# Batch 0's attention by halves of the tokens, with its states loaded by GpSimd's queue

## The chip, the cores and the metric

The kernel runs on one core of a Trainium2 chip. Its engines are TensorE (PE; PEld is its weight load), VectorE (DVE), ScalarE (ACT), GpSimd (POOL) and SyncE (SP), and 16 DMA engines serve the queues of SP, ACT and POOL. The metric is the device time of one execution in microseconds (us), median of several runs.

## The reference, cut to what matters

Two stages follow each other. First, for each of 8 batches and 8 heads, 512 tokens `x` and 32 states `state`, both of width 64, attend to each other in both directions. Then the result, 8 x (512 + 32) = 4352 rows of 512, goes through a wide layer with the activation h * erf(softplus(h)).

```python
# x: (8, 8, 512, 64), state: (8, 8, 32, 64); scale = 1/8
scores = scale * x @ state^T            # (B, H, 512, 32)
a = exp(scores - max over the 32); a /= sum + 1e-9
xread = a @ state                       # tokens read the states
scores2 = scale * state @ x^T           # (B, H, 32, 512)
a2 = exp(scores2 - max over the 512); a2 /= sum + 1e-9
sread = a2 @ x                          # states read the tokens
rows = concat(xread, sread)             # -> (4352, 512)
h = rows @ w_in                         # w_in (512, 2048), float64 in memory
g = h * erf(softplus(h))
out = g @ w_out                         # w_out (2048, 512), float64 in memory
```

Two things that the kernel does with this matter here. It never forms `xread`: it multiplies the states by `w_in` first (m = state @ w_in) and then the weights `a` by m. And it turns the float64 weights into float32 itself, on ScalarE and VectorE, piece by piece ("i" a piece of w_in, "o" a piece of w_out).

## The kernel before

Batch 0's tokens come in four chunks of 128, on two queues in turn, and the states follow on SP's queue. Then the first weight pieces are fetched, on SP as well.

```python
for c in range(NC):
    (nc.scalar, nc.sync)[c % 2].dma_start(
        out=x_t[0][:, c], in_=x[0, :, P * c:P * c + P].rearrange("h p d -> p h d"))
for e in range(2):
    nc.sync.dma_start(out=st[:, 0, D * e:D * e + D],
                      in_=state[0].rearrange("(i e) n d -> e i n d", e=2)[e])
```

`attention0` is the attention of batch 0. The tokens are turned on TensorE (so that the width lies on the partitions), copied from PSUM, multiplied by the states, turned back by VectorE, and become weights. `between` holds what is put between the steps.

```python
def attention0(between):
    xt = x_t[0]
    xT = att.tile([P, NI, S], F32, name="xT")
    xp = [ps_o.tile([P, S], F32, name="o%d" % i) for i in range(3)]
    xp.append(ps_h.tile([P, S], F32, name="h"))
    for c in 1, 0, 2, 3:
        if c == 2:
            warm(3)                      # filler products of the identity
        for i in range(NI):              # L304
            nc.tensor.transpose(out=xp[i][:, P * c:P * c + P],
                                in_=xt[:, c, 2 * i:2 * i + 2, :], identity=ident)
    for i in range(NI):                  # L307: 0 and 2 on ScalarE, 1 and 3 on VectorE
        (nc.scalar.copy, nc.vector.tensor_copy)[i % 2](xT[:, i, :], xp[i])
    states(range(1), ps_h, "h")          # turns the states (L182), copies them (L183)
    s2 = scored(0, xT)                   # L197: two PSUM tiles, one for each head of a pair
    between[0]()
    both = att.tile([P, NI, S], F32, name="xT")
    sc = att.tile([P, 2, S], F32, name="sc")
    a = states_weights(0, s2, both)      # L217 turn, L219 maximum, L221 subtract, L222 exp
    for e in range(2):
        nc.scalar.copy(sc[:, e], s2[e])
    between[1]()
    z1 = sums(a)                         # L228
    between[2]()
    normalise(a, z1)                     # L232, L233, L235
    for e in range(2):
        nc.vector.transpose(out=aT[0][:, e], in_=both[:, e])    # L321
    ...
```

A weight piece takes two passes on ScalarE (L144, L146) and three on VectorE (L147 to L149); `on_act` and `on_dve` place them, and the third VectorE pass lets the next piece be fetched. `mixed_part` forms m (L421, copies L423 and L424). `first0` (L714) multiplies m by the turned weights `aT[0]`: TensorE's first product for the wide layer. After it come `soft` (L718), `keep_h` (L721), `erf` (L724), `times` (L727) and the product with w_out (`some0`, L550).

```python
def after_scores():
    warm(32)
    on_act("i", 0)
def before_sums():
    on_act("i", 1)
    on_dve("i", 0, [0, 1])
def amid_sums():
    on_dve("i", 0, [2])
    on_act("o", 0, [0])
    m_t[0, 0] = mix.tile([P, 2, gw], F32, name="m")
    mixed_part(0, 0, 0, 2, nc.scalar.copy, nc.scalar.copy)
    warm(5)
rest = attention0((after_scores, before_sums, amid_sums))
...
first0(0, 0, g0[0])
first0(0, 1, g0[0])
on_dve("i", 1)
soft(0, g0)
...
```

For all of this `in_order` keeps the instructions of TensorE, VectorE, ScalarE and SP in the order of the program. GpSimd is left out of it: in the kernel before, it makes constants and the identity and nothing else.

Of the kernel before, what the change touches and what calls it, by code (L numbers as in the profile page):

```python
# [8 lines left out]
F32 = mybir.dt.float32  # L9
U32 = mybir.dt.uint32  # L10
ALU = mybir.AluOpType
ACTF = mybir.ActivationFunctionType
AX = mybir.AxisListType
# [3 lines left out]
def kernel(  # L17
# [17 lines left out]
    nc = tc.nc  # L35
    B, H, S, D = x.shape
    Ns = state.shape[2]
    d_model, d_ff = moe_w_in.shape
    P = 128
    NI = H // 2  # L40
    NC = S // P
# [5 lines left out]
    scale = 1.0 / (D ** 0.5)  # L47
# [4 lines left out]
    xin = ctx.enter_context(tc.tile_pool(name="xin", bufs=1))  # L52
    att = ctx.enter_context(tc.tile_pool(name="att", bufs=1))
    small = ctx.enter_context(tc.tile_pool(name="small", bufs=2))
    keep = ctx.enter_context(tc.tile_pool(name="keep", bufs=2))
# [3 lines left out]
    ps_at = ctx.enter_context(tc.tile_pool(name="ps_at", bufs=2, space=PSUM))  # L59
    ps_h = ctx.enter_context(tc.tile_pool(name="ps_h", bufs=2, space=PSUM))  # L60
    ps_o = ctx.enter_context(tc.tile_pool(name="ps_o", bufs=1, space=PSUM))

    ident = const.tile([P, P], F32, name="ident")
# [41 lines left out]

    st = const.tile([P, B, P], F32, name="st")
    x_t[0] = xin.tile([P, NC, H, D], F32, name="x")
    for c in range(NC):
        (nc.scalar, nc.sync)[c % 2].dma_start(
            out=x_t[0][:, c], in_=x[0, :, P * c:P * c + P].rearrange("h p d -> p h d"))  # L110
    for e in range(2):
        nc.sync.dma_start(out=st[:, 0, D * e:D * e + D],
                          in_=state[0].rearrange("(i e) n d -> e i n d", e=2)[e])

    def load_st():
        for h in range(H):
# [49 lines left out]
    def warm(n):  # L166

        for _ in range(n):
            last = nc.tensor.matmul(out=spare[:, 0:P], lhsT=ident, rhs=ident, start=True,
                                    stop=True)  # L170
        return last
# [3 lines left out]
    aT = {}  # L175

    def states(bs, pool=ps_at, name="at"):


        ps = pool.tile([P, len(bs), P], F32, name=name)  # L180
        for k, b in enumerate(bs):
            last = nc.tensor.transpose(out=ps[:, k], in_=st[:, b, :], identity=ident)  # L182
        nc.scalar.copy(st[:, bs[0]:bs[-1] + 1, :], ps)  # L183
        return last

    over = lambda t: t.unsqueeze(2).to_broadcast([P, NC * NI, Ns])
# [3 lines left out]
    def scored(b, xT):  # L190


        s2 = [ps_at.tile([P, S], F32, name="at") for _ in range(2)]
        for i in reversed(range(NI)):
            for e in range(2):
                r, q = slice(D * e, D * e + D), slice(Ns * i, Ns * i + Ns)
                on_pe = nc.tensor.matmul(out=s2[e][q, :], lhsT=st[r, b, q], rhs=xT[r, i, :],  # L197
                                         start=True, stop=True)
        marks.append(on_pe)
        return s2  # L200
# [10 lines left out]
    def states_weights(b, sc, both):  # L211

        aT[b] = keep.tile([P, 2, S], F32, name="aT")
        a = both[:, 0:2].rearrange("p e (k n) -> p e k n", n=Ns)
        m1 = small.tile([P, 2, NC * NI], F32, name="m1")
        for e in range(2):
            nc.vector.transpose(out=both[:, e], in_=sc[e])  # L217
        for e in range(2):
            nc.vector.reduce_max(out=m1[:, e], in_=a[:, e], axis=AX.X)  # L219
        for e in range(2):  # L220
            nc.vector.tensor_tensor(a[:, e], a[:, e], over(m1[:, e]), op=ALU.subtract)  # L221
            nc.scalar.activation(out=a[:, e], in_=a[:, e], func=ACTF.Exp, scale=scale)  # L222
        return a

    def sums(a):
        z1 = small.tile([P, 2, NC * NI], F32, name="z1")
        for e in range(2):
            nc.vector.reduce_sum(out=z1[:, e], in_=a[:, e], axis=AX.X)  # L228
        return z1

    def normalise(a, z1):
        nc.vector.tensor_scalar(z1, z1, 1e-9, None, op0=ALU.add)  # L232
        nc.vector.reciprocal(z1, z1)  # L233
        for e in range(2):
            nc.vector.tensor_tensor(a[:, e], a[:, e], over(z1[:, e]), op=ALU.mult)  # L235

    def largest(sc):
        m2 = small.tile([P, 2], F32, name="m2")
        for e in range(2):
            nc.vector.reduce_max(out=m2[:, e:e + 1], in_=sc[:, e], axis=AX.X)  # L240
        nc.vector.tensor_scalar(m2, m2, -scale, None, op0=ALU.mult)
        return m2

    def weigh_tokens(sc, m2, a2):

        z2 = small.tile([P, 2], F32, name="z2")
        for e in range(2):
            nc.scalar.activation(out=a2[:, e], in_=sc[:, e], func=ACTF.Exp, bias=m2[:, e:e + 1],
                                 scale=scale, accum_out=z2[:, e:e + 1])
        return z2  # L250

    def inverse(z):
        nc.vector.tensor_scalar(z, z, 1e-9, None, op0=ALU.add)
        nc.vector.reciprocal(z, z)

    def turn_weights(a2):
        a2T = att.tile([P, 2, NC, P], F32, name="sc")
        for e in range(2):
            ps = ps_at.tile([P, NC, P], F32, name="at")
            for c in range(NC):  # L260
                nc.tensor.transpose(out=ps[:, c, :], in_=a2[:, e, P * c:P * c + P],
                                    identity=ident)
            nc.scalar.copy(a2T[:, e], ps)
        return a2T
# [27 lines left out]
    def attention0(between):  # L292

        xt = x_t[0]
        xT = att.tile([P, NI, S], F32, name="xT")
        xp = [ps_o.tile([P, S], F32, name="o%d" % i) for i in range(3)]
        xp.append(ps_h.tile([P, S], F32, name="h"))
        for c in 1, 0, 2, 3:  # L300
            if c == 2:
                warm(3)
            for i in range(NI):
                nc.tensor.transpose(out=xp[i][:, P * c:P * c + P],  # L304
                                    in_=xt[:, c, 2 * i:2 * i + 2, :], identity=ident)
        for i in range(NI):
            (nc.scalar.copy, nc.vector.tensor_copy)[i % 2](xT[:, i, :], xp[i])  # L307
        states(range(1), ps_h, "h")
        s2 = scored(0, xT)
        between[0]()  # L310
        both = att.tile([P, NI, S], F32, name="xT")
        sc = att.tile([P, 2, S], F32, name="sc")
        a = states_weights(0, s2, both)
        for e in range(2):
            nc.scalar.copy(sc[:, e], s2[e])
        between[1]()
        z1 = sums(a)
        between[2]()
        normalise(a, z1)
        for e in range(2):  # L320
            nc.vector.transpose(out=aT[0][:, e], in_=both[:, e])  # L321

        def rest():
            a2 = both[:, 2:4]
            m2 = largest(sc)
            yield
            z2 = weigh_tokens(sc, m2, a2)
            inverse(z2)
            yield
            a2T = turn_weights(a2)  # L330
            yield
            read_tokens(0, a2T, z2)
            yield

        return rest()
# [304 lines left out]
    def begins(b):  # L640
        return 1 - b % 2
# [48 lines left out]
    def fetch():  # L690
        if len(made) < len(pieces):
            kind, j = w = pieces[len(made)]
            made[w] = (weights_in if kind == "i" else weights_out)(j)

    def on_act(kind, j, ks=range(2)):
        for k in ks:
            made[kind, j][0][k]()

    def on_dve(kind, j, ks=range(3)):
        for k in ks:  # L700
            made[kind, j][1][k]()
            if k == 2:
                fetch()
# [25 lines left out]
    def group():  # L729
        return [act.tile([P, 4, S], F32, name=n) for n in ("s", "hs")]  # L730
# [3 lines left out]
        fetch()  # L734
    warm(8)

    def after_scores():
        warm(32)
        on_act("i", 0)

    def before_sums():
        on_act("i", 1)
        on_dve("i", 0, [0, 1])

    def amid_sums():
        on_dve("i", 0, [2])
        on_act("o", 0, [0])
        m_t[0, 0] = mix.tile([P, 2, gw], F32, name="m")
        mixed_part(0, 0, 0, 2, nc.scalar.copy, nc.scalar.copy)
        warm(5)  # L750

    rest = attention0((after_scores, before_sums, amid_sums))
    g0 = group()

    def some0(g, gT, rs, ts):
# [112 lines left out]
    xT, _ = turn_x(1)  # L868
# [7 lines left out]
    turn = attention(1, xT)  # L876
# [40 lines left out]
    at = [combine_a(1)]  # L917
# [12 lines left out]
    for b in range(1, B + 1):  # L930
# [4 lines left out]
        for g, (first, second) in enumerate(groups):  # L935
# [5 lines left out]
            if b + 1 < B:  # L941

                late = b == 1
                if g == late:
                    side[6 if late else 6] = (lambda: behind(marks, next, turn)) if late else \
                        lambda old=turn: (next(old), behind(marks, next, turn))
                    turn = attention(b + 1)
# [6 lines left out]
                if g > 1:  # L954
                    o = g - 2 ^ begins(b + 1)
# [56 lines left out]
```

## Time and profile before

| | |
|---|---|
| median of 3 runs | 732.24 us (732.22 to 732.41) |
| profiled span | 730.7 us |
| first product of the wide layer (L714) | 22.10 us |
| first product with w_out (L550) | 31.01 us |
| first weight piece in use (ScalarE, L144) | 11.49 us |
| DMA of the first two chunks and states | 256 KB a chunk, 32 KB for each half of the states |

The busy line gives each engine's time, share of the span and instructions; the DMA line gives the busy share of the DMA engines in 40 slices of the span, in tenths. A timeline has one instruction or a merged run of the same kind per line: start, length, engine, source line, operation, tile written from tile read, and in brackets how long the engine had been idle before it and what released it. A float32 product appears as two instructions on TensorE, a transpose as one. Overlapping lengths are usual, since an engine takes up an instruction before the one ahead has ended; the distance between starts is what an instruction costs in a row of them.

### The profile page before, as it was taken

How to read it: one execution, taken by the hardware profiler on the slowest of the kernel's cores; microseconds unless marked ns; L12 is line 12 of the kernel's file. 1: busy time of each engine (PE TensorE's matmuls, PEld its weight loads, DVE VectorE, ACT ScalarE, POOL GpSimd, SP SyncE). 2: the span in 40 equal slices, each digit the busy share in tenths (PEclk: the TensorE clock that was granted, in tenths of full speed). 3: DMA queues.
4: the chain of work that ended last, by engine and by line, in shares of the span. 5: the costliest groups of instructions: out<-in, count | busy, mean ns of one | idle time of the engine just before them, and what ended most of it. 6: DMA issues, size and time to landing. Idle time of an engine off the chain costs nothing.

```text
span 730.7 us, 12128 instructions
## 1 busy us (share of the span) xinstructions
PE 721.6 (99%) x5016; PEld 588.0 (80%) x5016; DVE 524.0 (72%) x766; ACT 395.6 (54%) x498; POOL 0.7 (0%) x6
## 2 busy tenths in 40 slices
PE   8899999999999999999999999999999999999998
PEld 7434435889889888988989888988898899999996
DVE  4988887997798677867587669866686756674423
ACT  4898894665556444754455445544575434443340
POOL 0000000000000000000000000000000000000000
PEclk9999999999999999999999999999999999999999
DMA  7577842330153203310061104220111000000001
GB/s 234 174 216 241 224 94 58 87 59 30 19 99 67 50 1 66 80 30 30 1 144 27 33 1 94 60 44 9 38 50 30 30 1 30 1 30 1 30 1 29
DMA packets 139166, 46.40 MB, mean 64 GB/s; under 512 B 126696, under 2 KB 130536, under 8 KB 139112
## 3 DMA queue, kind: packets, MB, share of 16 engines
q1 hardware_dynamic: 136840, 44.92, 24.6%
q10 hardware_dynamic: 2272, 0.72, 0.5%
q8 instruction: 39, 0.64, 0.4%
q14 instruction: 15, 0.12, 0.1%
HBM read 33.03 MB, written 8.91 MB: 57 GB/s over the span
## 4 chain that ended last, share of the span: by engine, by line
PE 92%; DVE 2%; ACT 1%; issue 0%; ACTq 0%
PE o L600 50%; PE h L493 27%; PE o L550 7%; PE at L407 2%; PE h L407 1%; PE h L714 1%; PE at L197 1%; PE at L421 1%; PE h L277 1%; DVE s L727 0%; PE at L277 0%; DVE hs L721 0%; ACT L724 0%; DVE w_out L148 0%; ACT s L724 0%
## 5 line engine op out<-in xcount | busy, mean ns | idle before, releaser
L600 PE MATMUL o<-w_out,s 128*128 128x256 f32 x480 | 118.0, 380 | 0.0
L600 PE MATMUL o<-raw,hs 128*128 128x256 f32 x480 | 117.3, 382 | 0.0
L500 ACT ACTIVATE s<-hs 128x512 f32<-128x512 f32 x120 | 75.4, 630 | 74.3 <-DVE hs L501 74.0
L600 PE MATMUL o<-w_out,hs 128*128 128x256 f32 x480 | 114.1, 380 | 0.0
L600 PEld LDWEIGHTS o<-raw,hs 128*128 128x128 f32 x480 | 89.9, 190 | 22.6 <-issue 10.9
L501 DVE TENSOR_TENSOR hs<-hs,h 128x512 f32<-128x512 f32 x90 | 61.8, 687 | 62.6 <-PE h L493 62.4
L600 PEld LDWEIGHTS o<-w_out,hs 128*128 128x128 f32 x480 | 90.8, 190 | 16.3 <-issue 4.2
L600 PEld LDWEIGHTS o<-w_out,s 128*128 128x128 f32 x480 | 84.6, 191 | 7.9
L501 DVE TENSOR_TENSOR hs<-s,h 128x512 f32<-128x512 f32 x60 | 41.1, 685 | 67.6 <-PE h L493 67.1
L493 PEld LDWEIGHTS h<-aT,m 128*128 128x128 f32 x672 | 83.8, 192 | 4.3 <-issue 1.4
L493 PE MATMUL h<-aT,m 128*128 128x128 f32 x672 | 84.4, 275 | 0.0
L545 DVE TENSOR_TENSOR s<-s,hs 128x2048 f32<-128x2048 f32 (+1 forms) x31 | 68.8, 2218 | 20.4 <-ACT s L543 20.4
L504 ACT COPY s<-h 128x512 f32<-128x512 f32 x29 | 17.0, 585 | 107.7 <-PE h L493 107.7
L550 PE MATMUL o<-w_out,s 128*128 128x512 f32 x128 | 59.1, 600 | 0.6 <-DVE s L727 0.5
L493 PE MATMUL h<-sy,sx 128*128 128x128 f32 x448 | 59.4, 275 | 0.0
L493 PEld LDWEIGHTS h<-sy,sx 128*128 128x128 f32 x448 | 56.7, 192 | 2.1 <-issue 0.5
L543 ACT ACTIVATE s<-s 128x2048 f32<-128x2048 f32 x30 | 57.4, 1912 | 0.3
L509 ACT COPY hs<-h 128x512 f32<-128x512 f32 x29 | 17.0, 585 | 74.8 <-PE h L493 74.8
L600 PE MATMUL o<-raw,s 128*128 128x256 f32 x240 | 56.8, 379 | 0.0
L550 PEld LDWEIGHTS o<-w_out,s 128*128 128x128 f32 x128 | 23.1, 190 | 31.1 <-issue 25.8
L600 PEld LDWEIGHTS o<-raw,s 128*128 128x128 f32 x240 | 43.5, 190 | 4.7
L500 ACT ACT_TABLE_LOAD x31 | 39.8, 1283 | 0.5
(133 smaller groups left out, 915.4 us busy)
## 6 DMA issues: line engine op xcount, KB each, us to landing
raw<-in_moe_w_in_dram SPq DMA_DIRECT2D x8, 1024.0 KB, 5.7
raw<-in_moe_w_out_dram SPq DMA_DIRECT2D x8, 1024.0 KB, 4.8
xq<-in_x_dram SPq DMA_DIRECT2D x112, 64.0 KB, 2.2
x<-in_x_dram SPq DMA_DIRECT2D x56, 128.0 KB, 2.8
out_dram<-ot SPq DMA_DIRECT2D x18, 256.0 KB, 2.2
sc<-xT SPq DMA_DIRECT2D x112, 32.0 KB, 1.9
out_dram<-ot SPq DMA_DIRECT2D x28, 128.0 KB, 1.9
x<-in_x_dram ACTq DMA_DIRECT2D x2, 256.0 KB, 5.7
```

Source lines behind the costliest of these rows:

```text
L197: on_pe = nc.tensor.matmul(out=s2[e][q, :], lhsT=st[r, b, q], rhs=xT[r, i, :], start=True, stop=True)
L277: nc.tensor.matmul(out=sr[q, e, :], lhsT=a2T[:, e, c, q], rhs=xt[:, c, 2 * i + e, :], start=(c == 0), stop=(c == NC - 1))
L407: nc.tensor.matmul(out=ps[k][e][q, :], lhsT=st[r, b, q], rhs=w_in[r, 2 * g:2 * g + 2, i, :], start=True, stop=True)
L493: last = nc.tensor.matmul(out=bank[:, q], lhsT=lhsT, rhs=rhs, start=(first and i == 0 and k == 0), stop=(i == GF - 1 and k == len(ops) - 1 ...
L500: nc.scalar.activation(out=s[:, k], in_=hs[:, k], func=ACTF.Softplus)
L501: add = lambda o, x, y: nc.vector.tensor_tensor(o, x, y, op=ALU.add)
L504: copy(m1, p)
L509: copy(c11, p)
L543: nc.scalar.activation(out=s, in_=s, func=ACTF.Erf)
L545: nc.vector.tensor_tensor(s[:, k], s[:, k], hs[:, k], op=ALU.mult)
L550: nc.tensor.matmul(out=acc[r], lhsT=gT[:, i, P * r:P * r + P], rhs=w_out[:, GF * g + i, :], start=(g == 0 and i == 0), stop=(g == NG - 1 a ...
L600: nc.tensor.matmul(out=acc[bank][:, E2 * c:E2 * c + E2], lhsT=lhs[:, i, :], rhs=rhs[:, g, i, :], start=(first and i == 0 and c == 0), stop ...
```

## The change

The attention of batch 0 is done in two halves of 256 tokens, so that the first half's copies, scores and turning need only chunks 0 and 1. The states are asked for by GpSimd's queue rather than behind the tokens on SP. The turned tokens get a buffer of their own (that of `xq`, not yet in use), so that the turned scores of one half can be written while the tokens of the other are still read. The fillers' numbers and the places of the weight passes are changed to go with it.

```diff
+    for e in range(2):
+        nc.gpsimd.dma_start(out=st[:, 0, D * e:D * e + D],
+                            in_=state[0].rearrange("(i e) n d -> e i n d", e=2)[e])
     for c in range(NC):
         (nc.scalar, nc.sync)[c % 2].dma_start(...)
-    for e in range(2):
-        nc.sync.dma_start(out=st[:, 0, D * e:D * e + D], ...)
 ...
-        xT = att.tile([P, NI, S], F32, name="xT")
+        xT = xin.tile([P, NI, S // Ns, Ns], F32, name="xq").rearrange("p i m n -> p i (m n)")
 ...
+        def turn(t):          # chunks (1, 0) or (2, 3) into two PSUM tiles
+            xp = [ps_o.tile([P, 2, H2], F32, name="o%d" % (2 * t)),
+                  ps_h.tile([P, 2, H2], F32, name="h") if t else
+                  ps_o.tile([P, 2, H2], F32, name="o1")]
+            ...
+        def copies(t, xp):
+            nc.scalar.copy(xT[:, 0:2, cols[t]], xp[0])
+            nc.vector.tensor_copy(xT[:, 2:4, cols[t]], xp[1])
+        def score(t):         # 8 products of 256 tokens into two ps_at tiles
+            ...
+        def turn_scores(t, s2):
+            for e in range(2):
+                nc.vector.transpose(out=both[:, e, cols[t]], in_=s2[e])
+        def copy_scores(t, s2):
+            for e in range(2):
+                nc.scalar.copy(sc[:, e, cols[t]], s2[e])
+        def exps(t):
+            k = blocks[t]
+            nc.vector.reduce_max(out=m1[:, :, k], in_=a[:, :, k], axis=AX.X)
+            nc.vector.tensor_tensor(a[:, :, k], a[:, :, k], over(m1[:, :, k]), op=ALU.subtract)
+            nc.scalar.activation(out=a[:, :, k], in_=a[:, :, k], func=ACTF.Exp, scale=scale)
+        def sum_(t):
+            nc.vector.reduce_sum(out=z1[:, :, blocks[t]], in_=a[:, :, blocks[t]], axis=AX.X)
+
+        copies(0, turn(0))
+        states(range(1), ps_h, "h")
+        warm(1)
+        s0 = score(0)
+        xp = turn(1)
+        turn_scores(0, s0)
+        copy_scores(0, s0)
+        copies(1, xp)
+        warm(3)
+        s1 = score(1)
+        exps(0)
+        between[0]()          # warm(28), on_act("i", 0, [0])
+        turn_scores(1, s1)
+        exps(1)
+        between[1]()          # on_act("i", 0, [1])
+        copy_scores(1, s1)
+        sum_(0)
+        between[2]()          # on_dve("i", 0, [0])
+        sum_(1)
+        between[3]()          # on_act("i", 1), on_dve("i", 0, [1, 2]), on_act("o", 0, [0]),
+                              # mixed_part, warm(8)
         normalise(a, z1)
```

The comments to the right of the last calls are added here: they tell what the new `between` functions hold.

More of the change, by code (lines that the diff above doesn't have):

```diff
@@ L110 @@
             out=x_t[0][:, c], in_=x[0, :, P * c:P * c + P].rearrange("h p d -> p h d"))
-    for e in range(2):
-        nc.sync.dma_start(out=st[:, 0, D * e:D * e + D],
-                          in_=state[0].rearrange("(i e) n d -> e i n d", e=2)[e])
     def load_st():
@@ L292, in attention0 @@
     def attention0(between):
+        H2 = S // 2
+        NB = NC * NI // 2
         xt = x_t[0]
-        xT = att.tile([P, NI, S], F32, name="xT")
[L298 to L310, printed above, removed]
+        xT = xin.tile([P, NI, S // Ns, Ns], F32, name="xq").rearrange("p i m n -> p i (m n)")
         both = att.tile([P, NI, S], F32, name="xT")
         sc = att.tile([P, 2, S], F32, name="sc")
-        a = states_weights(0, s2, both)
-        for e in range(2):
-            nc.scalar.copy(sc[:, e], s2[e])
+        aT[0] = keep.tile([P, 2, S], F32, name="aT")
@@ new lines, in attention0 @@
+        a = both[:, 0:2].rearrange("p e (k n) -> p e k n", n=Ns)
+        m1, z1 = (small.tile([P, 2, NC * NI], F32, name=n) for n in ("m1", "z1"))
+        cols = [slice(H2 * t, H2 * t + H2) for t in range(2)]
+        blocks = [slice(NB * t, NB * t + NB) for t in range(2)]
+        over = lambda v: v.unsqueeze(3).to_broadcast([P, 2, NB, Ns])
+        def turn(t):
+            xp = [ps_o.tile([P, 2, H2], F32, name="o%d" % (2 * t)),
+                  ps_h.tile([P, 2, H2], F32, name="h") if t else
+                  ps_o.tile([P, 2, H2], F32, name="o1")]
+            for c in ((1, 0), (2, 3))[t]:
+                for i in range(NI):
+                    nc.tensor.transpose(out=xp[i // 2][:, i % 2, P * (c % 2):P * (c % 2) + P],
+                                        in_=xt[:, c, 2 * i:2 * i + 2, :], identity=ident)
+            return xp
@@ new lines, in copies @@
+        def copies(t, xp):
+            nc.scalar.copy(xT[:, 0:2, cols[t]], xp[0])
+            nc.vector.tensor_copy(xT[:, 2:4, cols[t]], xp[1])
+        def score(t):
+            s2 = [ps_at.tile([P, S], F32, name="at")[:, 0:H2] for _ in range(2)]
+            for i in range(NI):
+                for e in range(2):
+                    r, q = slice(D * e, D * e + D), slice(Ns * i, Ns * i + Ns)
+                    nc.tensor.matmul(out=s2[e][q, :], lhsT=st[r, 0, q], rhs=xT[r, i, cols[t]],
+                                     start=True, stop=True)
+            return s2
@@ new lines, in turn_scores @@
+        def turn_scores(t, s2):
+            for e in range(2):
+                nc.vector.transpose(out=both[:, e, cols[t]], in_=s2[e])
+        def copy_scores(t, s2):
+            for e in range(2):
+                nc.scalar.copy(sc[:, e, cols[t]], s2[e])
[4 more added lines that the diff above has]
+            nc.scalar.activation(out=a[:, :, k], in_=a[:, :, k], func=ACTF.Exp, scale=scale)
@@ L316, in attention0 @@
+        def sum_(t):
[14 more added lines that the diff above has]
+        exps(1)
         between[1]()
-        z1 = sums(a)
+        copy_scores(1, s1)
@@ L735, with amid_scores, amid_exps, amid_sums @@
     warm(8)
[L737 to L741, printed above, removed]
+    def amid_scores():
+        warm(28)
+        on_act("i", 0, [0])
+    def amid_exps():
+        on_act("i", 0, [1])
+    def amid_sums():
+        on_dve("i", 0, [0])
+    def behind_sums():
         on_act("i", 1)
-        on_dve("i", 0, [0, 1])
-    def amid_sums():
-        on_dve("i", 0, [2])
+        on_dve("i", 0, [1, 2])
         on_act("o", 0, [0])
@@ L749, in amid_sums @@
         mixed_part(0, 0, 0, 2, nc.scalar.copy, nc.scalar.copy)
-        warm(5)
-    rest = attention0((after_scores, before_sums, amid_sums))
+        warm(8)
+    rest = attention0((amid_scores, amid_exps, amid_sums, behind_sums))
     g0 = group()
```

## The prediction

> **What bounds the kernel now.** I read the page first, then the timeline of each engine for the first 40 us, then the waits of TensorE, VectorE and ScalarE, and last the DMA queues in half-microsecond slices. The busy table and the slices say where nothing can be won:
>
> ```profile
> PE 721.6 (99%) x5016; PEld 588.0 (80%) x5016; DVE 524.0 (72%) x766; ACT 395.6 (54%) x498; POOL 0.7 (0%) x6
> ...
> DMA  7577842330153203310061104220111000000001
> ```
>
> TensorE is busy all through, but in the first 22 us a good part of that is filler (`warm`, L169, products of the identity that nobody reads). Its first product of the long pipeline is `first0`, L714, in VectorE's and TensorE's timelines:
>
> ```profile
> 8.86 0.69 DVE L307 COPY xT<-o 128x512 f32<-128x512 f32 x1 [8.86 <-PE o L304]
> 9.47 0.68 DVE L307 COPY xT<-h 128x512 f32<-128x512 f32 x1
> 11.57 1.31 DVE L217 STREAM_TRANSPOSE xT<-at 128x512 f32<-128x512 f32 x2 [1.42 <-PE at L197]
> 12.81 1.24 DVE L219 TENSOR_REDUCE m<-xT 128x16 f32<-128x512 f32 x2
> 13.96 1.28 DVE L221 TENSOR_TENSOR xT<-xT,m 128x512 f32<-128x512 f32 x2
> ...
> 20.04 1.29 DVE L235 TENSOR_TENSOR xT<-xT,z 128x512 f32<-128x512 f32 x2
> 21.25 1.30 DVE L321 STREAM_TRANSPOSE aT<-xT 128x512 f32<-128x512 f32 x2
> 22.47 0.65 DVE L147 TENSOR_SCALAR w_in<-w_in 128x1024 uint32<-128x1024 uint32 x1
> ```
>
> The columns are start, length, engine, line, operation. No bracket stands between 11.57 and 22.47: **VectorE works without a pause** through batch 0's attention and the conversion of the first weight block. It goes on so until 36.53, where its timeline shows its next wait. So the prologue ends when VectorE has done its list, and the list begins late: at 8.86 for the copies, then a 1.42 us hole. TensorE's timeline shows why:
>
> ```profile
> 6.64 0.98 PE L169 MATMUL o<-ident 128*128 128x128 f32 x6
> 7.95 0.55 PE L304 MATMUL o<-ident,x 128*128 128x128 f32 x3 [0.32 <-DMA x<-in_x_dram]
> ...
> 9.22 0.30 PE L182 MATMUL h<-ident,st 128*128 128x128 f32 x1 [0.18 <-DMA st<-in_state_dram]
> 10.30 1.09 PE L197 MATMUL at<-xT,st 64*32 64x512 f32 x16 [0.78 <-DVE xT L307]
> ...
> 22.10 3.67 PE L714 MATMUL h<-aT,m 128*128 128x512 f32 x8 [0.33 <-DVE aT L321]
> ```
>
> Token chunks 1 and 0 are turned from 4.92 to 6.85, but nothing may be copied before chunks 2 and 3 are there (7.95), since one PSUM tile holds all four. And the states, queued on SP behind chunk 3, were the last thing waited for at 9.22.
>
> **After the prologue** TensorE waits for little: its waits from 31 to 110 us sum to 0.7 us, and from 110 us it is busy in 30.00 of 30.00 and 60.00 of 60.00 us. A head start of the prologue should therefore arrive at the end nearly whole, and nothing else in the change can matter.
>
> **What the Trainium skill says.** "DMA: Bandwidth & Descriptors", section "Issuing engines are not separate DMA queues": DMAs of all issuing engines run on the same 16 engines and interleave. The trace agrees: SP's queue (q1) and ACT's (q10) trade the lead, 160 against 414 packets in 3.5 to 4 us, 390 against 42 in 4.5 to 5. The same page, "Specifications", gives a first byte after about 1 us for GpSimd's software path against 0.6 us for SP's; no DMA of this kernel is issued there, so no run here shows it yet. "SBUF — State Buffer", "Who interferes with whom", warns that VectorE in a two-port mode locks GpSimd out while it writes descriptors. VectorE's first instruction here is at 8.86 us, and about 7 in the new order, so that should not bite. "TensorE: Matmul & The Clock Gate", Part 1: an idle TensorE runs at half clock until some 3.4 us of work. This trace agrees: four transposes take 0.87 us at 4.92 and 0.49 us at 7.95.
>
> **The change, part by part.**
>
> *1. States by GpSimd.* Two DMAs of 32 KB, 128 packets of 256 B each. Now they stand behind chunk 3 on q1: small packets other than ACT's number 16, 69, 111, 74 and 10 in the half-microseconds from 6.0 to 8.5 us, among the first weights' 2 KB packets. The last were gone soon after 8, and 9.1 for landing fits the wait at 9.22 (chunk 1's 1024 packets were gone near 4.0 and landed 4.83, so some 0.8 us go by after the last packet). GpSimd is free at 1.30. With 1 us for the first byte of each and the same 0.8 us for landing I estimate 4 to 6 us. The 256 packets only change place: at 850 to 1150 packets per us they push the four chunks back by at most 0.3 us.
>
> *2. Turning and scoring by halves.* My estimate of the new order, each duration from a row above or its half:
> - Chunks 1 and 0 turned by 6.9; ScalarE's and VectorE's copies of 512 columns 7.1 to 7.8 (0.69 as before).
> - States turned behind them (0.30), copied by ScalarE (0.28) behind its xT copy: 7.9.
> - `score(0)`: 16 matmul instructions of 256 columns. The 512 form took 1.09; L421, of the same 64x32 tiling and 256 columns, took 0.67 to 0.79 with its tail. So 8.05 to 8.75.
> - `turn(1)`: chunk 2 landed 7.95; 8 transposes 1.1, so 8.75 to 9.75.
> - Beside it VectorE turns half the scores, two of 256 columns. I take 0.36 each, a little over half of 0.65. Done at 9.7. ScalarE copies them out (0.38 each, as the 256-column L423).
> - VectorE's `copies(1)` starts near 9.9.
>
> *3. VectorE's list from there.* By start-to-start distances of before: copy 0.61, maximum 0.58, subtraction 0.60, two half transposes 0.72, maximum 0.58, subtraction 0.60, sum 0.58, first weight step 0.82, sum 0.58, second 1.14, third 1.13, z 0.60, product 1.21, transposes 1.22. The sum is 10.97, ending at 20.9, against 22.47 now. The total work is not smaller: same instruction sizes, with four transposes in place of two (+0.1 to 0.2). **What is won is where it lies**, in the hole before 11.57. Gain by this list: 1.6 us at best.
>
> *4. ScalarE as partner.* Exponentials of half 0 at 12.1 (0.6), first weight pass 12.7 to 13.8, exponentials of half 1 at 14.0, second pass 14.6 to 15.6, the scores' copy, then three weight passes of 1.05 to about 19.5, and the copies of m at 20.2. All stand just ahead of VectorE's use. Only the second pass is tight (VectorE wants it near 15.6), and I charge 0.1 to 0.2.
>
> *5. Fillers.* 28 pairs of L169 at 7.41/64 = 0.116 us each make 6.5 us; 8 make 1.86. Between `score(1)` (end about 11.5) and the product with w_in (about 18.2) there are 6.7 us, and then about 2.4 to `first0`, so they fit without delaying.
>
> Sum: 1.6 less 0.1 to 0.2 for ScalarE, less 0.1 to 0.3 for x landing later: a gain of about 1.2 us at `first0`, carried to the end. 732.24 - 1.2 = 731.0; I round towards the rivals, 731.1.
>
> **The rivals.**
> - *Chunk 2 becomes the wait.* SP's weights are issued about 1.5 us sooner, with no states between, and can take slots from ACT's last chunk (q10 fell from 408 to 17 packets per half-microsecond as the weights began). If chunk 2 lands at 9 rather than 8, `turn(1)` and `copies(1)` slip by 0.5 and the gain is 0.6: 731.6. For it: packets of 2 KB against 256 B in turn. Against: chunk 2 was issued at about 1.3, ahead of any weight.
> - *GpSimd's states come late.* TensorE's order puts the states before both scores and the second half's turning, so a landing at 9 instead of 5 holds up everything, as now: gain 0 to 0.3, 732.1. Against: GpSimd is idle from 1.3.
> - *ScalarE becomes the bound.* Its list is full from 12 to 20. One pass of 1.1 us out of step costs up to 0.6: 731.7.
> - *The start is given back.* From 22 to 31 us TensorE waits on VectorE and ScalarE together: ScalarE's erf ends at 29.64, VectorE's product starts at 29.71, and L550 starts at 31.01 behind it. If the weights' transfers held these, little would be left. Against: their issues wait on VectorE (L149, 33.6 us of waits), so they move along.
> - *A half-speed TensorE.* It pauses at 7.3 to 8.0, just when it speeds up; a delay there would stretch `score(0)` and `turn(1)` by about 0.7.
>
> **Range and chances.** The rivals take back 0.4 to 1.2 of 1.2 us; two at once, or a fixed cost of GpSimd's queue that I can't see, would lose a little. A better landing of x could bring 1.8. So 730.3 to 732.5. Two per cent is 14.6 us: no step here comes near it.
>
> **What would show it.** Right: `first0` (L714) starts at about 20.9; the states' transpose runs near 7; VectorE's first copy is at about 7, and its list has no wait over 0.3 us from the second copy on; PE's later waits are as before. Wrong: a wait of TensorE for st or x after 8.5, VectorE waiting for ScalarE's weight pass, or `first0` early but the first L550 still at 31.

## The result and the profile after

The change made the kernel slower: 734.99 us against 732.38, medians of six runs each. The ratio of the means, which all ratios below are, is 1.0037 (95% interval 1.0024 to 1.0050). The prediction was 731.1 us with a range of 730.3 to 732.5, so the sign was wrong as well.

The page after, the engines' busy time and the DMA slices, hardly differs:

```profile
PE 721.7 (98%) x5032; PEld 588.0 (80%) x5032; DVE 524.7 (72%) x768; ACT 396.1 (54%) x500; POOL 2.1 (0%) x8
...
DMA  7577752330043202410061104220121000000001
```

The timelines do differ. TensorE's, with the columns as before (L315 turns the tokens, L182 the states, L328 is the scores by halves, L764 is `first0`):

```profile
6.11 1.11 PE L315 MATMUL o<-ident,x 128*128 128x128 f32 x8
9.91 0.45 PE L182 MATMUL h<-ident,st 128*128 128x128 f32 x1 [2.69 <-DMA st<-in_state_dram]
10.15 0.63 PE L169 MATMUL o<-ident 128*128 128x128 f32 x2
10.72 1.11 PE L328 MATMUL at<-xq,st 64*32 64x256 f32 x16
11.75 0.69 PE L315 MATMUL o<-ident,x 128*128 128x128 f32 x2
12.24 0.63 PE L315 MATMUL h<-ident,x 128*128 128x128 f32 x2
12.66 0.59 PE L315 MATMUL o<-ident,x 128*128 128x128 f32 x2
...
24.53 3.62 PE L764 MATMUL h<-aT,m 128*128 128x512 f32 x8
```

The first half's tokens are turned by 7.2, and then **TensorE waits 2.69 us for the states**. Before, it had other work in that time (fillers, chunks 2 and 3) and waited 0.18. Behind the wait, four transposes take 0.91 us (starts 11.75 to 12.66); before, four of chunk 2 took 0.49 (7.95 to 8.44). VectorE's timeline has the hole that the halves were to fill, now larger:

```profile
7.26 0.69 DVE L321 COPY xq<-o 128x512 f32<-128x512 f32 x1 [7.26 <-PE o L315]
11.91 0.78 DVE L334 STREAM_TRANSPOSE xT<-at 128x256 f32<-128x256 f32 x2 [3.96 <-PE at L328]
13.51 0.69 DVE L321 COPY xq<-h 128x512 f32<-128x512 f32 x1 [0.81 <-PE h L315]
14.12 0.68 DVE L342 TENSOR_REDUCE m<-xT 128x16 f32<-128x512 f32 x1
14.83 0.69 DVE L343 TENSOR_TENSOR xT<-xT,m 128x512 f32<-128x512 f32 x1
...
24.84 0.65 DVE L147 TENSOR_SCALAR w_in<-w_in 128x1024 uint32<-128x1024 uint32 x1
```

The second half's copies were predicted near 9.9 and start at 13.51; from there to the end of its list at 24.84 VectorE has no wait. From 31 to 110 us TensorE's waits sum to 0.7 us, as before. So `first0` comes 2.43 us later (24.53 - 22.10) and the profiled execution is 2.5 us longer (734.94 against 732.44).

Why the transposes are slow stands in the table of windows of TensorE: window and its length, busy time (instructions), **granted clock**, DMA share, GB/s.

```profile
5.00:10.00 5.00, 2.31 (x16) 0.97 1.16 281
10.00:12.00 2.00, 2.00 (x20) 0.50 1.05 409
12.00:14.00 2.00, 2.00 (x14) 0.73 1.07 432
14.00:16.00 2.00, 2.00 (x28) 1.00 0.63 250
```

In the kernel before, the clock is 1.00 in all of these windows. The half-speed stretch follows the wait.

### The profile page after: what moved, and what is told of

The parts are those of the page before. It is cut to its first block, busy times and chain, and to the rows that moved or that the text cites. A ratio compares the mean times of both kernels' runs of the same rounds, so it can differ in the third digit from the quotient of the medians.

```text
span 733.2 us, 12162 instructions
## 1 busy us (share of the span) xinstructions
PE 721.7 (98%) x5032; PEld 588.0 (80%) x5032; DVE 524.7 (72%) x768; ACT 396.1 (54%) x500; POOL 2.1 (0%) x8
## 4 chain that ended last, share of the span: by engine, by line
PE 88%; DVE 4%; ACT 1%; SPq 1%; issue 1%; DMA 0%; DVEq 0%; ACTq 0%
PE o L650 47%; PE h L543 27%; PE o L600 7%; PE at L457 2%; SPq L432 1%; PE h L457 1%; PE h L764 1%; PE at L197 1%; PE at L471 1%; PE h L277 1%; DVE s L777 0%; PE at L277 0%; DVE hs L771 0%; ACT L774 0%; DVE w_out L148 0%
```

## The experiments

Each kernel below ran beside the kernel before on the same chip. "Halves" means the changed kernel.

**1. The two parts alone.** `h_sp`: halves, with the states back on SP behind the tokens.

```diff
-    for e in range(2):
-        nc.gpsimd.dma_start(out=st[:, 0, D * e:D * e + D], ...)
     for c in range(NC): ...                     # tokens as before
+    for e in range(2):
+        nc.sync.dma_start(out=st[:, 0, D * e:D * e + D], ...)
```

> The changed kernel with the states back on SP's queue behind the tokens: the halves alone. Theory 1 (the states' landing on GpSimd's queue at 9.8 us sets everything): they land near 9.1 as in the kernel before, the states are turned at 9.2, the second half's copies start near 12 instead of 13.5, first0 (L764) at about 23.0 instead of 24.53, and the time is near 733.2. Theory 2 (the identity, made 1.2 us later behind GpSimd's first DMA, leaves TensorE at half speed): the same 9.2, but transposes of the second half at 0.12 us each instead of 0.21, so first0 near 22.2 and 732.4. Theory 3 (halves cost more than they save): first0 stays over 24, 734.5 or more.

Measured: 735.07 us, ratio 1.0035 (1.0022 to 1.0049), mean granted clock 0.994 to 0.995. One execution of five, the profiled one, took 1933.89 us and is left out, so its trace is not read. The time is that of theory 3, but the low clock keeps it from being put down to the halves by themselves: it points to the same half-speed stretch as in the change, which without a trace is argued and not shown. The run does show that taking the states off GpSimd's queue is not enough, as on SP they stand behind chunk 3; in the kernel before, that meant turning them at 9.22.

`q_pool`: the kernel before, with the states on GpSimd's queue ahead of the tokens.

> The kernel before with the states on GpSimd's queue: the queue alone. Theory 1: the states land near 9.8, are turned at 9.9 instead of 9.22, the scores start near 10.8 instead of 10.30, and 0.5 to 0.7 us are lost: about 733.0. Theory 2: a late identity and a slow TensorE lose more, 1.5 us or above: 734. Theory 3: the queue costs nothing here, 732.4.

Measured: 733.13 us, ratio 1.0013 (1.0006 to 1.0019). The size is theory 1's, the way is not: its states do not hold TensorE up, chunk 2 does. Its TensorE timeline:

```profile
8.60 0.55 PE L304 MATMUL o<-ident,x 128*128 128x128 f32 x3 [0.61 <-DMA x<-in_x_dram]
...
9.53 0.27 PE L182 MATMUL h<-ident,st 128*128 128x128 f32 x1
```

8.60 against 7.95 before is the 0.65 by which its `first0` is late (22.75 against 22.10). SP now issues the weights from 1.86 (3.45 before), and the last chunk to land came 7.3 us after its issue (6.7 before). How much of that is the weights' doing and how much the states' is not split here.

**2. The states early, by SP and ACT.** `h_mid`: halves, the states between the first and the second chunk of each queue.

```diff
+    for c in range(2):
+        (nc.scalar, nc.sync)[c % 2].dma_start(...)          # chunks 0, 1
+    for e in range(2):
+        (nc.scalar, nc.sync)[e].dma_start(out=st[:, 0, D * e:D * e + D], ...)
+    for c in range(2, NC):
+        (nc.scalar, nc.sync)[c % 2].dma_start(...)          # chunks 2, 3
```

> The changed kernel with the states on SP's and ACT's queues, one half of them each, between the first and the second chunk of tokens. Theory 1: they land by 6.5 and TensorE no longer waits for them; the second half's copies start near 10, first0 at about 21.0, the time 731.1 as first predicted. Theory 3: first0 later than 22.1, 732.4 or more. If chunk 2 is pushed back by the small packets, first0 about 21.5 and 731.6.

Measured: 734.72 us, ratio 1.0029 (1.0021 to 1.0036). The states came as expected, and the next wait took the place of theirs:

```profile
6.57 0.30 PE L185 MATMUL h<-ident,st 128*128 128x128 f32 x1
6.71 0.39 PE L172 MATMUL o<-ident 128*128 128x128 f32 x2
7.23 0.75 PE L331 MATMUL at<-xq,st 64*32 64x256 f32 x16
11.17 0.69 PE L318 MATMUL o<-ident,x 128*128 128x128 f32 x2 [3.20 <-DMA x<-in_x_dram]
```

Chunk 2, last on ACT's queue, landed 8.7 us after its issue. Its queue still moved 159, 106 and 65 packets in the microseconds from 7, 8 and 9, while SP's weights took 88 to 100% of the engines' time. The clock fell here too (0.50 from 10 to 16 us).

**3. The identity.** GpSimd's first DMA slipped between the two instructions that make the identity, and TensorE's first filler started at 2.54, not 1.35. `h_ident` binds both DMAs behind the identity:

```diff
     make_identity(nc, ident)
+    identity_made = nc.cur_bb.bb.instructions[-1]
 ...
+        tc.add_manual_dep(asked.ins, identity_made.name, ...)   # order only, no wait
```

> The changed kernel, with GpSimd's two DMAs bound to come after the identity is made, not between its two instructions. Theory 1: the states land no earlier (9.8), so nothing is won or at most 0.4 us: 734.6 to 735. Theory 2: with the identity at 1.3 TensorE starts its fillers 1.2 us sooner and keeps its speed; transposes of the second half at 0.12 us each, and 1 to 1.5 us are won: 733.6.

Measured: 734.85 us, ratio 1.0028 (1.0017 to 1.0038), so theory 1: the late identity isn't the cause. The spread tells more. The executions lasted 732.62 to 735.13 us; the shortest, which is the profiled one, had a mean clock of 1.000, the two longest 0.995. In the profiled one the states were turned at 8.76 after a wait of 1.91, the clock stayed up, and `first0` came at 22.18.

**4. The clock alone.** `h_fill` puts fillers into the wait and leaves the states as late as they are.

```diff
         copies(0, turn(0))
+        warm(12)
         states(range(1), ps_h, "h")
```

> The changed kernel with 12 more fillers of TensorE between the turning of the first half and the states, where it now waits 2.7 us for their landing. Theory 1 (the late states alone): the fillers only fill a wait, first0 stays near 24.5 and the time at 735.0. Theory 2 (the wait lets the granted clock of TensorE fall to 0.5 for some 3 us, which doubles the second half's turning and scores): the clock stays at 1.0 throughout, the states are still turned near 9.9, but first0 comes at about 23.2 and the time is near 733.6.

Measured: 733.95 us, against 734.99 for the change, nearer to theory 2. The times alone would not settle it: the ratio to the kernel before is 1.0028 (1.0016 to 1.0039), against 1.0037 (1.0024 to 1.0050), as one execution of six took 736.19. The trace does. The windows of its TensorE:

```profile
5.00:10.00 5.00, 5.00 (x37) 1.00 1.18 277
10.00:12.00 2.00, 1.87 (x28) 1.00 1.05 408
12.00:14.00 2.00, 1.88 (x29) 1.00 1.06 426
```

Three lines of its timelines:

```profile
10.24 0.27 PE L182 MATMUL h<-ident,st 128*128 128x128 f32 x1
12.60 0.69 DVE L321 COPY xq<-h 128x512 f32<-128x512 f32 x1 [0.20 <-PE h L315]
23.61 3.62 PE L765 MATMUL h<-aT,m 128*128 128x512 f32 x8
```

The states are turned at 10.24 here, 0.33 later than in the change, and yet `first0` comes at 23.61, 0.92 sooner. From the states' turning to the second half's copies it takes 2.36 us at full clock (10.24 to 12.60) and took 3.60 (9.91 to 13.51). **The pause costs 1.2 us beyond its own length.**

**5. Why the states land late.** `alone`: all tokens wait for the states.

```diff
+    for c in range(NC):
+        nc.scalar.copy(x_t[0][:, c, 0, 0:8], st[:, 0, D - 4:D + 4])   # then overwritten
```

> The changed kernel with all tokens held back until the states have landed (ScalarE writes eight columns of each chunk from the states first), so that GpSimd's two DMAs have only the weights' traffic beside them at the start. If GpSimd's path itself takes its time, they still land 6.5 to 7.5 us after issue. If the tokens' 256-byte packets hold them up, 2 to 3 us after issue. The whole is slower, as the tokens come later: some 738 us.

Measured once: 737.62 us. The states' time from issue to landing, first in the change, then in `alone` (the view of the tile `st`):

```profile
DMA to landing us min/median/max: 6.7/7.0/7.4
```

```profile
DMA to landing us min/median/max: 2.3/2.4/2.5
```

The path itself needs 2.4 us. (Nor do the weights run yet in `alone`: they stand behind the tokens on SP, so it shows the path with nothing beside it.) The DMA queues of the change between 6 and 7 us, and of `alone` between 2 and 3, by packets, MB and share of the engines:

```profile
q10 hardware_dynamic: 508, 0.13, 83.4%
q0 software_dynamic: 47, 0.03, 19.2%
q1 hardware_dynamic: 28, 0.05, 32.2%
```

```profile
q0 software_dynamic: 37, 0.02, 15.3%
```

GpSimd's two DMA instructions had ended by 3.11 us in the change, but its queue (q0) moved no packet before 6 us, when SP's tokens were through; a second batch, 45 of its 96 packets, came between 8 and 9. VectorE cannot have held it up until 6 us: its first instruction starts at 7.26.

`h_hold`: the change, with the first weights held until the tokens are there, by GpSimd writing a few words of their buffer from chunks 2 and 3.

```diff
         raw = act.tile([P, 2 * shape[0] * i], U32, name="raw", bufs=3)
+        if not fetched:
+            for c in 2, 3:
+                nc.gpsimd.tensor_copy(raw[:, 8 * c:8 * c + 8].bitcast(F32), x_t[0][:, c, H - 1, D - 8:D])
```

> The changed kernel with its first weight pieces held back until all tokens have landed (their buffer is written by GpSimd from chunks 2 and 3 first). If the weights on SP's queue are what keeps the states and chunk 2 late: the states land 1 us sooner or more (near 8.5), first0 at 23 or before, 733.5. If the states wait for something else (GpSimd's own path, or the tokens' packets): they land at 9 to 9.8 as before, and the time stays near 735.

Measured: 732.47 us, ratio 1.0002 (0.9994 to 1.0010). The states landed 6.0 to 6.8 us after issue, TensorE waited 0.51 for them, the clock stayed up, and `first0` came at 22.02. So the weights add 0.6 us to the states' landing, and the tokens' packets, with 2.4 alone and 6.4 here in the median, some 4 us. Even so it only draws level with the kernel before.

**6. An order of loading that suits the halves.** Three kernels keep all last chunks on SP, ahead of the weights.

```text
 h_sp3:    SP: chunks 1, 2, 3, weights               ACT: chunk 0, states
 h_early:  SP: half the states, chunks 1, 2, 3, ...  ACT: half the states, chunk 0; warm(4) for warm(1)
 h_early1: as h_early, with the change's warm(1)
```

> The changed kernel with token chunks 1, 2 and 3 on SP's queue, so that no weights get ahead of any chunk, and chunk 0 and then the states on ACT's queue. If the landing of states and of chunk 2 are the whole cause: all land by 8, TensorE has no wait over 1 us, its clock stays at 1.0, first0 at about 21.0 and the time 731.1 to 731.4, faster than the kernel before. If halves themselves cost: first0 over 22.1 and over 732.4 even so.

Measured: 733.89 us, ratio 1.0020 (1.0011 to 1.0028). Chunk 2 is no longer waited for, but the states are, for 1.85 us to 8.08, and in 12 of 13 executions the mean clock is 0.998 or less. The one at 1.000 took 731.66.

> The changed kernel with both causes taken away: the states first of all, one half on SP's queue and one on ACT's, then chunk 0 on ACT's and chunks 1, 2 and 3 on SP's, so that no weight is ahead of any of them; and 4 fillers instead of 1 ahead of the first half's scores. If late landings and the clock are the whole cause: states land by 5, chunk 2 by 8.3, no wait of TensorE over 0.7 us, clock 1.0, second half's copies at 10, first0 at 21.1 and 731.4 (11.1 us from those copies to first0, as in the other kernels by halves). If something else in the halves costs: 732.3 or more.

Measured: 731.76 us, ratio 0.9996 (0.9988 to 1.0004), not clear of noise. `first0` came at 21.42: the states ahead of the tokens put the first chunks back, and TensorE waited 1.33 for them at 6.28.

> The same with the one filler of the changed kernel ahead of the first half's scores. If a pause of TensorE of about 1 us does not lower its clock: the same time within 0.2 us. If it does: 1 us more, with the clock below 1.0 near 10 us.

Measured: 731.56 us, ratio 0.9994 (0.9986 to 1.0002). The executions of both lie in two groups, 731.1 to 731.9 and 732.5 to 733.8, with clocks of 0.999 to 1.000; what the fillers add here is not settled. Nor does the wait tell the groups apart. The profiled execution of h_early1 is of the slower one (732.56), that of h_early of the faster (731.94). The turning of the first half and its scores, h_early first:

```profile
6.28 1.46 PE L315 MATMUL o<-ident,x 128*128 128x128 f32 x8 [1.33 <-DMA x<-in_x_dram]
8.66 0.66 PE L328 MATMUL at<-xq,st 64*32 64x256 f32 x16
```

```profile
5.70 2.14 PE L315 MATMUL o<-ident,x 128*128 128x128 f32 x8 [0.57 <-DMA x<-in_x_dram]
8.41 1.29 PE L328 MATMUL at<-xq,st 64*32 64x256 f32 x16
```

h_early1 waits for less (0.57 us) and starts sooner, but its scores take 1.29 us instead of 0.66, and its `first0` comes at 22.08. Its clock record reads 1.00 all the while.

`b_early`: the kernel before with h_early's order of loading.

> The kernel before with that same order of loading: no halves. If halves are what an early landing is worth something with, little is won, as the whole block waits for the last chunk (7.95 before): 731.9 to 732.4. If the order of loading does it alone: 731.4.

Measured: 733.05 us, ratio 1.0015 (1.0009 to 1.0022), slower: without halves the order brings nothing. All four chunks are turned later, from 6.31 against 4.92 before, and `first0` comes at 22.59.

`h_next`: halves, chunk 0 alone on ACT; on SP chunk 1, states, chunks 2 and 3, weights.

```diff
+    chunk(0, nc.scalar)
+    chunk(1, nc.sync)
+    for e in range(2):
+        nc.sync.dma_start(out=st[:, 0, D * e:D * e + D], ...)
+    chunk(2, nc.sync)
+    chunk(3, nc.sync)
 ...
-        warm(1)
+        warm(3)
         s0 = score(0)
```

> The changed kernel with chunk 0 alone on ACT's queue, and on SP's chunk 1, the states, chunks 2 and 3 and then the weights; 3 fillers instead of 1 ahead of the first half's scores. The first chunks are not delayed by the states, the states not by the last chunks, and no chunk by the weights. If the earlier runs are read rightly: TensorE turns from 4.9, states land by 6.9, no wait over 0.7 us, clock 1.0, second half's copies at 9.8, first0 11.1 us later at 20.9, and the time 731.1: faster than the kernel before by 0.1 to 0.2 per cent, clear of noise. If the loading order cannot bring this: first0 after 21.5 and 731.7 or more.

Measured: **730.66 us, ratio 0.9977 (0.9968 to 0.9986)**, faster than both. Its TensorE:

```profile
4.93 1.42 PE L319 MATMUL o<-ident,x 128*128 128x128 f32 x8
6.51 0.30 PE L186 MATMUL h<-ident,st 128*128 128x128 f32 x1 [0.16 <-DMA st<-in_state_dram]
6.64 0.83 PE L173 MATMUL o<-ident 128*128 128x128 f32 x6
7.41 0.66 PE L332 MATMUL at<-xq,st 64*32 64x256 f32 x16
8.00 0.44 PE L319 MATMUL o<-ident,x 128*128 128x128 f32 x2
...
20.15 3.61 PE L768 MATMUL h<-aT,m 128*128 128x512 f32 x8
```

No wait over 0.16 us from the turning of the tokens to the end of the first scores, the clock at 1.00, and `first0` 1.95 us sooner than before. The slowest chunk landed 4.9 us after its issue. The second half's copies start at 9.13, against the 9.9 that the prediction had worked out for landings of this kind. The kernel before was not run with this order, so how the 1.69 us (732.35 to 730.66) divide between order and halves is not shown.

## Why the prediction was wrong, by its own steps

**Carried to the end: right.** In each profiled execution but that of h_sp I take the time less the start of `first0`:

| kernel | first0 | time | difference |
|---|---|---|---|
| before | 22.10 | 732.44 | 710.34 |
| the change | 24.53 | 734.94 | 710.41 |
| q_pool | 22.75 | 733.24 | 710.49 |
| h_mid | 24.77 | 734.91 | 710.14 |
| h_ident | 22.18 | 732.62 | 710.44 |
| h_fill | 23.61 | 734.00 | 710.39 |
| h_hold | 22.02 | 732.53 | 710.51 |
| h_sp3 | 22.79 | 733.05 | 710.26 |
| h_early | 21.42 | 731.94 | 710.52 |
| h_early1 | 22.08 | 732.56 | 710.48 |
| b_early | 22.59 | 732.90 | 710.31 |
| alone | 27.24 | 737.62 | 710.38 |
| h_next | 20.15 | 730.48 | 710.33 |

710.1 to 710.5, whatever was done in the prologue. The rival of a start given back falls.

**The landing of the states, 4 to 6 us: the step that failed.** They were waited for until 9.91. I had added a first byte's delay and 0.8 us for landing, which is enough for a queue by itself (2.4 us in `alone`), and taken for granted that 256 packets in company with 4096 only "change place". The trace counts 96 and not 256, and they did not get their turns: none moved in the change while both other queues carried tokens (in h_hold, 8 did). The Trainium skill, "DMA: Bandwidth & Descriptors", section "Queues, rings and completion order", says that a DMA engine goes round the queues that have work, packet by packet. For SP and ACT the trace of h_mid agrees at first: 158 and 159 packets from 7 to 8 us. But turns are not bytes: a turn of the weights moved 2 KB and one of the tokens 256 B (0.32 against 0.04 MB), so the last chunk on ACT fell behind. For GpSimd's queue the change disagrees: from 4 to 6 us it moved nothing, and the other two 1813 packets. Why it got no turn stays open.

The rival "GpSimd's states come late" named the landing (9 instead of 5) but put its cost at no gain, "as now". It missed that the change makes the states needed sooner: before, they came last in TensorE's order, behind four chunks; now they come behind two, and score, second turning and copies stand behind them. A landing that was harmless is then a 2.7 us wait. Three pairs of kernels that share an order of loading show the same in their medians (the fillers differ too):

| order of loading | whole block | halves |
|---|---|---|
| states on SP behind the tokens | 732.38 | 735.07 (h_sp) |
| states by GpSimd | 733.13 (q_pool) | 734.99 (the change) |
| states first, chunks 1 to 3 on SP | 733.05 (b_early) | 731.76 (h_early) |

So the halves lost 1.9 to 2.7 us where the states came late, and won 1.3 where they came early.

**The clock: the second failure.** I named it as a rival of 0.7 us at a pause of 0.7 us, and left it out of the sum, because the pause that I foresaw was short. The pause was 2.69 us and the cost 1.2. "TensorE: Matmul & The Clock Gate", Part 1, ties the fall to an idle window of some 3.4 us. Here the fall went with shorter waits, of 3.20 (h_mid), 2.69 (the change) and 1.85 us (h_sp3), but not with one of 1.91: the profiled execution of h_ident kept its clock. Of the executions without a trace only the mean clock is known, not the wait: it was 0.998 or less in the other five of the change and the other seven of h_ident. The prediction's own reading of that page, half clock until some 3.4 us of work, was too short for these traces: the kernel before works from 1.35, and at 5.79 four transposes still take 0.85 us.

The three terms close the account for the copies of the second half: predicted 9.9, late states +2.9 (9.91 against 7.0), slow clock +1.2, and 0.5 less, as the work between the two takes 2.4 us at full clock and I had 2.9. The sum is 13.5, and 13.51 was measured. It closes by construction, since the last two terms both come from h_fill's 2.36 us; what h_fill tests is that the 1.2 us go when the pause is filled.

**VectorE's list: right but for its size.** I had 10.97 us from those copies to the end of the last transposes; it took 11.33 (13.51 to 24.84). In the halves a reduction is followed at once by the subtraction that needs it, 0.71 us from start to start where two reductions in a row had stood 0.58 apart. With the copies at 10.91, as in h_hold, such a list ends at 22.34, 0.13 us before that of the kernel before: it only drew level.

**Chunk 2 becomes the wait: a sound rival at the wrong place.** It set q_pool and h_mid, not the change, where the states came later still. ScalarE never became the bound: VectorE has no wait for it in the change before 24.84.

## What to carry to other kernels

Work that is moved forward moves the moment at which all its operands are needed: list each operand's landing, and load in the order in which they are now needed, with nothing large on another queue that can overtake them. A small transfer on a queue of its own can be the last to land when the other queues are full. And where the array's speed hangs on being busy, fill a wait with work even if nothing can be gained in the wait itself: 12 fillers brought `first0` of the changed kernel forward by 0.92 us (its median time by 1.0).

## What was not expected of the hardware

GpSimd's two transfers of 32 KB took 2.3 to 2.5 us with nothing beside them and 6.7 to 7.4 us beside the tokens. The granted clock in the profile does not show every slow stretch: in `alone`, after a wait of 4.91 us, eight transposes took 1.94 us (the last eight of the kernel before: 1.09, from 7.95 to 9.04) in a window whose clock reads 1.00. h_early1 is another such case. What decides whether a pause of about 2 us lowers the clock was not settled, nor how long TensorE stays slow at the start.
